# Three edits to where ScalarE's side work runs, between attention and mixing, in a fused attention, expert and mixing kernel

## The chip, the cores and the metric

The kernel runs on one core of one Trainium2 chip. The metric is the device time of one execution in microseconds (us). A core has a matrix engine (TensorE, PE in the rows), a vector engine (VectorE, DVE), a scalar engine (ScalarE, ACT), a general engine (GpSimd, POOL), and queues that issue transfers (SP's and ACT's are used here). Each engine works through its own list of instructions in the order in which they stand there; an instruction waits until what it reads is written and the buffer it writes is free, and everything behind it on its engine waits with it. TensorE writes into eight PSUM banks, which VectorE or ScalarE must read before a bank can be written again.

## The reference

Three layers follow each other: banded attention (4 batches, 8 heads, 576 positions), a mixture of 4 single-head experts over 512 channels, and a mixing layer. The change lies where the second ends and the third begins:

```
ye = a @ v @ wo[e]                       # per expert, weighted and added: x
theta = x @ w_theta
zr, zi = x * cos(theta), x * sin(theta)
y = einsum('ts,bsd->btd', w_tok_r, zr) + einsum('ts,bsd->btd', w_tok_i, zi)
u = x + y
out = u + maximum(u @ w_ch, 0)
```

The weights `w_theta`, `w_tok_*` and `w_ch` arrive as 64-bit floats and are turned into 32-bit ones on the chip.

## The kernel before

Everything is in single precision: each operand of a product is split into a high and a low part, and `mm3` (L99 to L102) issues three matmuls for one product (high by high L100, high by low L101, low by high L102). The work of a stage is written as generators that `merge` interleaves, and a scheduler then sets the final order of each engine's list from that program and its own estimate of durations; a different placement of a few instructions therefore moves many others.

The names the prediction needs, in order of time:

- `attn` (L419): expert attention of one batch and one pair of experts, in five query tiles t = 0 to 4. Scores go to bank `bs`, VectorE takes the row minimum (L452), ScalarE the exponential (L457); the scaling by the row sum and the gate (L469: `bms`, and `bpd` for the last block) is done on VectorE for one expert and on GpSimd for the other while t < 4 in the last batch. TensorE transposes the result (L480 into `bpt`, L486 into `bdt`), the copies L482 (VectorE), L484 and L490 (ScalarE) bring it back as `bpT`, and L156, L159, L498 form `o`.
- `wo` (L506): the output product of a batch into a bank `x`, eight banks per batch (two column ranges, 320 and 256 wide, by four blocks m), each copied out at L514: in batches 2 and 3 into the staging tiles `xs`, from where the SP queue writes them to DRAM. All eight copies of batch 3 are on ScalarE.
- `load64` (L107): the conversion of 64-bit weights, called with kind 0 (theta), 1 (token weights, `wtuk`, from `w64k`), 2 (channel weights, `wtuc`, from `w64c`). Its steps: first step `t` (L124 on GpSimd for kind 0, L127 on ScalarE for kinds 1 and 2), `u` (L129, ScalarE), a shift (L130) and a merge of bits (L136) on VectorE, an integer add on GpSimd (L138), the cast of the high part (L143, ScalarE) and the low part (L144: GpSimd for kind 1, VectorE for kind 2). Of nine token weights, numbers 5 to 8 are loaded late, on ScalarE's queue (L112), into two buffers in turn. `late[0]` is set in `attn(3, 1)` at t = 2 and marks the loads behind it.
- `closed[0]` is the last ScalarE cast of `attn` (L500); with kind 2 the ScalarE steps L127 and L129 are held until it has been issued.
- `theta` (L626): per batch, half and token tile i: product `th` in a `bs` bank, a transposed `x` as `xk` in a `tb` bank (L644), rounding (L648, L649, which frees `th`), sine and cosine on ScalarE (L651 to L653), the product with `xk` on VectorE (L656, which frees `xk`), and a split into `z` (high by ScalarE, low by GpSimd, L94 and L97; `cast[0]` holds the latest ScalarE half).
- `mix` (L674): `y` = `z` times token weights, four banks, nine steps c; VectorE adds each bank into `x2T` (L694). `channel` (L810) is the last product, `c`.

The stretch of the change is 276 to 345 us: `attn(3, 1)` ends, `wo(3)`, `theta(0, 0)` and then `mix(0, 0)` start. What follows until the end is the same mixing and channel work for the other halves and batches.

Of the kernel before, what the change touches and what calls it, by code (L numbers as in the profile page):

```python
# [22 lines left out]
B, H, S, D = 4, 8, 576, 64  # L23
DM = H * D
# [33 lines left out]
def kernel(ctx, tc, qT, kT, vw, consts, w_in, w_o, w_th, w_tk, w_ch, outT):  # L58
    nc = tc.nc
# [30 lines left out]
    cast = [None]  # L90
# [16 lines left out]
    def load64(kind, st, tu, dst_h, dst_l, src, scale=1.0):  # L107
# [12 lines left out]
        full = lo, hi, tu[:, 0], tu[:, 1], dst_h, dst_l  # L120
        for k in range(n):
            lo, hi, t, u, dst_h, dst_l = (x[:, step * k : step * k + step] for x in full)
            if KN["DM"][kind]:
                nc.gpsimd.tensor_scalar(out=f32(t), in0=f32(hi), scalar1=2.0**-112, scalar2=1.0, op0=ALU.mult, op1=ALU.mult)  # L124
            else:
                with tc.issue_after(closed[0].ins) if kind == 2 else nullcontext():
                    nc.scalar.mul(out=f32(t), in_=f32(hi), mul=2.0**-112)  # L127
            with tc.issue_after(closed[0].ins) if kind == 2 else nullcontext():
                nc.scalar.mul(out=u, in_=lo, mul=2.0**-29)  # L129
            shift = lambda: nc.vector.tensor_scalar(out=t, in0=t, scalar1=3, scalar2=None, op0=ALU.logical_shift_left)  # L130
            if kind == 1 and gated[0]:
                with tc.issue_after(gated[0].ins):
                    shift()
            else:
                shift()
            nc.vector.scalar_tensor_tensor(out=t, in0=hi, scalar=0x80000000, in1=t,  # L136
                                           op0=ALU.bitwise_and, op1=ALU.bitwise_or)
            nc.gpsimd.tensor_add(out=t.bitcast(I32), in0=t.bitcast(I32), in1=u.bitcast(I32))  # L138
            if scale == 1.0:
                if KN["DH"][kind]:  # L140
                    nc.vector.tensor_copy(out=dst_h, in_=f32(t))
                else:
                    nc.scalar.copy(out=dst_h, in_=f32(t))  # L143
                (nc.vector if KN["DL"][kind] else nc.gpsimd).tensor_sub(out=dst_l, in0=f32(t), in1=f32(dst_h))  # L144
            else:
                nc.scalar.activation(out=dst_h, in_=f32(t), func=AF.Copy, scale=scale)
                nc.vector.scalar_tensor_tensor(out=dst_l, in0=f32(t), scalar=scale, in1=f32(dst_h),
                                               op0=ALU.mult, op1=ALU.subtract)
# [357 lines left out]
    def wo(b):  # L506
        for n0, n1 in ((0, 320), (320, 576)):
            for m in range(NC):
                g = bank([P, n1 - n0], ("gggg", ("as", "ta", "g", "g"), ("as", "g", "ta", "g"))[KN["WB"][b]][m], f"x2{b}{m}{n0}")
                for c in range(2):  # L510
                    oh, ol = O[b, c]
                    mm3(g, woh[c][:, m * P : (m + 1) * P], wol[c][:, m * P : (m + 1) * P],
                        oh[:, n0:n1], ol[:, n0:n1], c == 0, c == 1)
                nc.scalar.copy(out=x2T[b][:, m, n0:n1] if b < 2 else xs[b][m // 2][:, m % 2, n0:n1], in_=g)  # L514
                if b > 1 and n1 == S and m % 2:
                    nc.sync.dma_start(xd[b][:, m - 1 : m + 1], xs[b][m // 2])
                yield 0.75
# [108 lines left out]
    def theta(b, dh):  # L626
        x2 = x2T[b]
        dsl = slice(dh * HW, dh * HW + HW)
        for i in range(4 if b % 2 else 5):
# [24 lines left out]
            if i < 4:  # L654
                both = ang[:, i % 2]
                d = nc.vector.tensor_mul(out=both, in0=xk.unsqueeze(1).to_broadcast([P, 2, HW]), in1=both)  # L656
                if 2 * b + dh < 3:
                    zt = slot(first[8 * b + 4 * dh + i], [P, 2, 2, HW], f"z{n}")
                    Z[b, dh, i] = zt
                    mark[b, dh, i] = d, split(zt[:, :, 0], zt[:, :, 1], both, nc.scalar, nc.gpsimd)  # L660
                elif i % 2:
                    mark[b, dh, i] = d, sums_of(b, dh, i, ang.rearrange("p j q (k n) -> p j q k n", k=2))
            else:
# [351 lines left out]
```

## Time and profile before

| what | us |
|---|---|
| runs of the kernel | 510.03, 509.95, 506.78 (median 509.95) |
| the profiled execution | 506.32 |
| its span, first to last instruction | 504.5 |
| busy in the span: TensorE | 480.7 |
| VectorE | 373.6 |
| ScalarE | 346.4 |
| GpSimd | 328.4 |

The rows further down come from the profiled execution, with times counted from the span's start. A timeline row gives start, duration, engine, line, operation and operands, and in brackets how long the engine had been idle before it and what it then waited for. A matmul's duration is its pipelined latency; successive matmuls start closer together than that. The waits view sums such idle time by pair of instructions.

### The profile page before, as it was taken

Reading aid. Unit: us, or ns where it says so; the run is one execution under the profiler, and the core shown is the slowest. Engines: PE = TensorE matmul, PEld = TensorE weight load, DVE = VectorE, ACT = ScalarE, POOL = GpSimd, SP = SyncE. Lnnn points to the kernel's source line nnn. Section 1 sums busy time; section 2 is a strip of 40 time slices with the busy share of each in tenths; the row PEclk is TensorE's granted clock in tenths of the full one; section 3 lists DMA queues with packets and bytes.
Section 4 is the critical chain, followed back from the end, with each engine's and each line's share of the span. In section 5 each row is a group of like instructions: output and inputs, shape, how many; then the busy total and the mean of one; then the engine's idle time right before and its main releaser. Section 6 shows DMA issues by size and latency. Waiting matters only on the chain.

```text
span 504.5 us, 12104 instructions
## 1 busy us (share of the span) xinstructions
PE 480.7 (95%) x4128; PEld 446.4 (88%) x4128; DVE 373.6 (74%) x1274; ACT 346.4 (69%) x1072; POOL 328.4 (65%) x455
## 2 busy tenths in 40 slices
PE   7798999999999999999999989999999999999997
PEld 5688888889998999988878778899998999999997
DVE  5766887865977868845897778987769948894942
ACT  7948787866787868858696797886177727652620
POOL 6758899764685772335784367579658926891770
PEclk9999999999999999999999999999999999999999
DMA  7564233431335342111246953231272044202002
GB/s 256 189 212 155 83 123 114 130 114 64 122 88 177 124 141 78 34 47 49 52 146 208 318 166 142 55 93 43 76 196 64 23 142 131 64 23 95 1 0 95
DMA packets 45470, 55.92 MB, mean 111 GB/s; under 512 B 6497, under 2 KB 34145, under 8 KB 45409
## 3 DMA queue, kind: packets, MB, share of 16 engines
q1 hardware_dynamic: 44544, 52.46, 33.1%
q10 hardware_dynamic: 864, 2.69, 1.5%
q8 instruction: 33, 0.54, 0.4%
q14 instruction: 29, 0.23, 0.2%
HBM read 43.34 MB, written 11.80 MB: 109 GB/s over the span
## 4 chain that ended last, share of the span: by engine, by line
PE 51%; DVE 20%; ACT 11%; POOL 9%; issue 5%; DMA 4%; SPq 0%; POOLq 0%; DVEq 0%; ACTq 0%
PE as L279 4%; PE bpt L480 3%; PE qk L100 2%; PE c L100 2%; DMA w64k<-in_dram 2%; PE qk L101 2%; PE apt L304 2%; PE c L102 2%; PE qk L102 2%; PE c L101 2%; ACT ams L292 2%; PE ao L159 2%; DMA wst<-in_dram 2%; PE bs L448 2%; DVE ang L656 2%
## 5 line engine op out<-in xcount | busy, mean ns | idle before, releaser
L292 ACT ACTIVATE ams<-ams,anm 128x128 f32<-128x128 f32 x144 | 56.6, 396 | 6.1 <-DVE anm L284 4.8
L299 POOL TENSOR_TENSOR ams<-ams,arc 128x384 f32<-128x384 f32 x48 | 40.1, 836 | 24.9 <-DVE arc L298 15.5
L87 POOL TENSOR_SCALAR QD<-qt 64x192 f32<-64x192 f32 x72 | 40.1, 557 | 19.1 <-PE as L279 11.6
L457 ACT ACTIVATE bms<-bms,bnm 64x64 f32<-64x64 f32 (+4 forms) x80 | 44.8, 562 | 9.3 <-DVE bnm L452 8.8
L279 PE MATMUL as<-kt,QD 128*128 128x128 f32 x288 | 41.9, 282 | 3.9 <-DVE anm L284 1.5
L284 DVE CUSTOM_DVE_ANT_0 ams<-as,cst 128x128 f32<-128x128 f32 x144 | 35.0, 284 | 11.5 <-PE apt L304 7.8
L279 PEld LDWEIGHTS as<-kt,QD 128*128 128x128 f32 x288 | 36.6, 193 | 7.4 <-ACT x0h L94 1.5
L452 DVE CUSTOM_DVE_ANT_0 bms<-bs,mb 64x64 f32<-64x64 f32 (+4 forms) x80 | 32.6, 424 | 7.5 <-PE bs L450 4.7
L469 POOL TENSOR_SCALAR bpd<-bms,bsm,gw 128x64 f32<-128x64 f32 (+1 forms) x47 | 21.9, 467 | 23.1 <-DVE bsm L462 10.6
L97 POOL TENSOR_TENSOR cu<-x2T,cu 128x288 fp32r<-128x288 f32 x32 | 29.1, 923 | 7.3 <-ACT cu L94 7.3
L100 PE MATMUL y<-wkh,z 128*128 128x288 f32 x108 | 32.1, 302 | 0.2 <-DVE x2T L694 0.2
L448 PE MATMUL bs<-KA,QS 128*128 128x288 f32 (+4 forms) x96 | 31.8, 340 | 0.4 <-DVE bnm L452 0.2
L101 PE MATMUL y<-wkl,z 128*128 128x288 f32 x108 | 31.9, 297 | 0.0
L102 PE MATMUL y<-wkh,z 128*128 128x288 f32 x108 | 31.3, 297 | 0.0
L768 POOL TENSOR_TENSOR x2T<-x2T,u 128x288 f32<-128x288 f32 x20 | 16.6, 839 | 21.3 <-DVE u L779 11.1
L480 PE MATMUL bpt<-cst,bms 128*128 128x128 f32 x160 | 27.6, 278 | 2.9 <-POOL bms L469 1.8
L648 ACT ACTIVATE ang<-th,magic 128x256 f32<-128x256 f32 x36 | 16.7, 466 | 17.9 <-PE th L102 17.5
L656 DVE TENSOR_TENSOR ang<-xk,ang 128x512 f32<-128x512 f32 x32 | 21.7, 684 | 8.2 <-ACT ang L653 6.2
L450 PE MATMUL bs<-KL,QS 128*128 128x288 f32 (+4 forms) x96 | 27.6, 295 | 0.1
L292 ACT ACTIVATION_READ_ACCUMULATOR ams<-ams,anm 128x1 f32 x144 | 27.5, 191 | 0.0
L820 DVE SCALAR_TENSOR_TENSOR x2T<-c,x2T 128x288 f32<-128x288 f32 x32 | 13.9, 453 | 16.5 <-PE c L102 16.3
L469 POOL TENSOR_SCALAR bms<-bms,bsm,gw 128x384 f32<-128x384 f32 (+3 forms) x40 | 25.4, 636 | 0.0
(336 smaller groups left out, 2040.5 us busy)
## 6 DMA issues: line engine op xcount, KB each, us to landing
vt<-in_dram SPq DMA_DIRECT2D x48, 192.0 KB, 3.1
or<-od SPq DMA_DIRECT2D x32, 256.0 KB, 3.3
kt<-in_dram SPq DMA_DIRECT2D x15, 320.0 KB, 3.1
qt<-in_dram SPq DMA_DIRECT2D x16, 288.0 KB, 3.4
out_dram<-x2T SPq DMA_DIRECT2D x32, 144.0 KB, 1.8
w64k<-in_dram SPq DMA_DIRECT2D x5, 576.0 KB, 3.7
od<-oh SPq DMA_DIRECT2D x8, 288.0 KB, 3.2
od<-ol SPq DMA_DIRECT2D x8, 288.0 KB, 4.1
```

What stands on the lines that cost most here:

```text
L87: nc.gpsimd.tensor_scalar(out=out, in0=in_, scalar1=by, scalar2=1.0, op0=ALU.mult, op1=ALU.mult)
L100: nc.tensor.matmul(out, wh, xh, start=first, stop=False)
L101: nc.tensor.matmul(out, wh, xl, start=False, stop=False)
L102: nc.tensor.matmul(out, wl, xh, start=False, stop=last)
L279: nc.tensor.matmul(s[:, i, :], QD[g][:, i], kt[:, 64 * blk : 64 * blk + 128], start=True, stop=True)
L284: nc.vector.tensor_tensor_reduce(out=ms[:, i, :], in0=s[:, i, :], in1=ma0 if (g == 0 and i == 0) else ma1, scale=-0.125, scalar=3.0e38, op ...
L292: nc.scalar.activation(out=ms[:, i, :], in_=ms[:, i, :], func=AF.Exp, bias=nm[:, i : i + 1], scale=-1.0, accum_out=sm[:, i, 0:1],)
L299: nc.gpsimd.tensor_mul(out=ms, in0=ms, in1=rc.unsqueeze(2).to_broadcast([P, 3, P]))
L448: nc.tensor.matmul(s[:m, : z - a], qs[:, q0 : q0 + m], ka[:, a:z], start=True, stop=False)
L457: ex = nc.scalar.activation(out=ms[:m, :w], in_=ms[:m, :w], func=AF.Exp, bias=nm[:m, ci : ci + 1], scale=-1.0, accum_out=ss[:m, i, 0:1])
L469: eng.tensor_scalar(out=dst, in0=src, scalar1=sm[:m, i : i + 1], scalar2=gw[:m, t, 2 * ep + i : 2 * ep + i + 1], op0=ALU.mult, op1=ALU.mult)
L480: nc.tensor.transpose(pt[:, jj, i, :], pn[:, i, P * j : P * j + P], ident)
```

## The change

Three edits. Of batch 3's eight output copies, the four with odd m go to VectorE. The late token weights (numbers 5 to 8) take their first step on GpSimd in place of ScalarE. And `closed[0]` is set once more at the split of the fourth tile of the first theta, so that the ScalarE steps of the channel weights' conversion are held until the cast of that `z` has been issued; before, they were held only behind the last attention cast.

```
-            if KN["DM"][kind]:
+            if KN["DM"][kind] or late[0] and kind == 1:
                 nc.gpsimd.tensor_scalar(out=f32(t), in0=f32(hi), scalar1=2.0**-112, scalar2=1.0, op0=ALU.mult, op1=ALU.mult)
             else:
                 with tc.issue_after(closed[0].ins) if kind == 2 else nullcontext():
...
-                nc.scalar.copy(out=x2T[b][:, m, n0:n1] if b < 2 else xs[b][m // 2][:, m % 2, n0:n1], in_=g)
+                dst = x2T[b][:, m, n0:n1] if b < 2 else xs[b][m // 2][:, m % 2, n0:n1]
+                if b == B - 1 and m % 2:
+                    nc.vector.tensor_copy(out=dst, in_=g)
+                else:
+                    nc.scalar.copy(out=dst, in_=g)
...
                     mark[b, dh, i] = d, split(zt[:, :, 0], zt[:, :, 1], both, nc.scalar, nc.gpsimd)
+                    if (b, dh, i) == (0, 0, 3):
+                        closed[0] = cast[0]
```

The engines' lists are alike up to the end of attention and differ from there on. Lines behind the new ones have moved: the copies of L514 are L516 (VectorE) and L518 (ScalarE) in the changed kernel, L656 is L660, L649 is L653, L644 is L648.

GpSimd while attention's last tiles run, before (`wtuk_4932` to `wtuk_4962` are the late token weights 5 to 8; `bpd_4829` and `bms_4827` are tile t = 3 of `attn(3, 1)`):

```order
L144 TENSOR_TENSOR wkl_4665<-wtuk_4932,wkh_4661 128x576
L138 TENSOR_TENSOR wtuk_4942<-wtuk_4942 128x576
L469 TENSOR_SCALAR bpd_4829<-bms_4827,bsm_4828,gw_4204 128x64
L469 TENSOR_SCALAR bms_4827<-bms_4827,bsm_4828,gw_4204 128x384
L138 TENSOR_TENSOR wtuk_4952<-wtuk_4952 128x576
```

and in the changed kernel:

```order
L144 TENSOR_TENSOR wkl_4665<-wtuk_4932,wkh_4661 128x576
L124 TENSOR_SCALAR wtuk_4952<-w64k_4951 128x576
L138 TENSOR_TENSOR wtuk_4942<-wtuk_4942 128x576
L469 TENSOR_SCALAR bpd_4829<-bms_4827,bsm_4828,gw_4204 128x64
L469 TENSOR_SCALAR bms_4827<-bms_4827,bsm_4828,gw_4204 128x384
L138 TENSOR_TENSOR wtuk_4952<-wtuk_4952 128x576
```

The first step of token weight 7 now stands ahead of the scaling of tile 3; two more such steps stand earlier, one later.

TensorE at the transposes of that same tile 3, before (`bpt_4849` and `bpt_4855` are its two banks; the first two transposes read VectorE's expert, the others GpSimd's; `x` is `wo(3)`, `th` is theta):

```order
L100 MATMUL x_4994<-oh_4265,woh_88 128x320
L101 MATMUL x_4994<-ol_4266,woh_88 128x320
L102 MATMUL x_4994<-oh_4265,wol_90 128x320
L480 MATMUL bpt_4849<-cst,bms_4827 128x128
L480 MATMUL bpt_4855<-cst,bms_4827 128x128
L480 MATMUL bpt_4849<-cst,bms_4827 128x128 x3
L480 MATMUL bpt_4855<-cst,bms_4827 128x128
```

and in the changed kernel, from the third of the twelve matmuls that now stand between the two pairs on:

```order
L100 MATMUL x_4994<-oh_4265,woh_88 128x320
L101 MATMUL x_4994<-ol_4266,woh_88 128x320
L102 MATMUL x_4994<-oh_4265,wol_90 128x320
L100 MATMUL x_4994<-oh_4671,woh_89 128x320
L100 MATMUL th_5105<-wot,or_4975 128x256
L101 MATMUL th_5105<-wot,or_4975 128x256
L102 MATMUL th_5105<-wot,or_4975 128x256
L100 MATMUL th_5105<-wot,or_4975 128x256
L101 MATMUL th_5105<-wot,or_4975 128x256
L102 MATMUL th_5105<-wot,or_4975 128x256
L480 MATMUL bpt_4849<-cst,bms_4827 128x128 x3
L480 MATMUL bpt_4855<-cst,bms_4827 128x128
```

Of the twelve, six are 320 columns wide and six 256; three of them stood ahead of the transposes before.

VectorE where the first theta's products are made, before (`ang` times `xk` is L656; `wtuc_5226` and `wtuc_5258` are the first two pieces of the channel weights):

```order
L656 TENSOR_TENSOR ang_5014<-xk_5011,ang_5014 128x512
L97 TENSOR_TENSOR ol_4672<-o_4917,oh_4671 128x128
L130 TENSOR_SCALAR wtuc_5226<-wtuc_5226 128x256
L136 SCALAR_TENSOR_TENSOR wtuc_5226<-w64ca,wtuc_5226 128x256
L656 TENSOR_TENSOR ang_5014<-xk_5091,ang_5014 128x512
L130 TENSOR_SCALAR wtuc_5258<-wtuc_5258 128x256
L136 SCALAR_TENSOR_TENSOR wtuc_5258<-w64ca,wtuc_5258 128x256
L656 TENSOR_TENSOR ang_5115<-xk_5112,ang_5115 128x512
L656 TENSOR_TENSOR ang_5115<-xk_5134,ang_5115 128x512
```

and in the changed kernel:

```order
L660 TENSOR_TENSOR ang_5014<-xk_5011,ang_5014 128x512
L97 TENSOR_TENSOR ol_4672<-o_4917,oh_4671 128x128
L660 TENSOR_TENSOR ang_5014<-xk_5091,ang_5014 128x512
L516 COPY xs3a<-x_5056 128x256
L516 COPY xs3b<-x_5073 128x256
L660 TENSOR_TENSOR ang_5115<-xk_5112,ang_5115 128x512
L660 TENSOR_TENSOR ang_5115<-xk_5134,ang_5115 128x512
L130 TENSOR_SCALAR wtuc_5226<-wtuc_5226 128x256
L136 SCALAR_TENSOR_TENSOR wtuc_5226<-w64ca,wtuc_5226 128x256
L130 TENSOR_SCALAR wtuc_5258<-wtuc_5258 128x256
L136 SCALAR_TENSOR_TENSOR wtuc_5258<-w64ca,wtuc_5258 128x256
```

Four instructions of the conversion left the row of products, two output copies came in.

## Rows read from the trace of the kernel before

**Rows 1.** Waits of TensorE, 276 to 345 us: total, times, longest
```profile
PE bpt L480 <- POOL bms L469: 1.3, 1, 1.3
PE xk L644 <- DVE ang L656: 1.1, 1, 1.1
PE th L100 <- DVE ang L649: 0.7, 1, 0.7
...
PE y L100 <- DVE x2T L694: 0.2, 1, 0.2
```

**Rows 2.** Waits of TensorE, 345 us to the end: first and last of six
```profile
PE c L100 <- DVE zf L670: 1.3, 1, 1.3
...
PE ya L100 <- DVE x2T L694: 0.3, 1, 0.3
```

**Rows 3.** Windows: us, busy time of PE, PEld, DVE, ACT, POOL, clock, DMA
```profile
276.00:310.00 34.00, 31.02 (x225) 26.16 (x222) 26.36 (x64) 28.93 (x74) 18.35 (x18) 1.00 0.65 227
310.00:328.00 18.00, 17.13 (x132) 16.71 (x131) 17.33 (x30) 13.90 (x39) 11.26 (x12) 1.00 0.19 57
```

**Rows 4.** Prices: one line's instructions, min/median/max ns, first and last start
```profile
L514 ACT COPY xs3a<-x x4: 425/433/467, 300.1 to 306.6; 128x320 f32<-128x320 f32 x2, 128x256 f32<-128x256 f32 x2
L127 ACT ACTIVATE wtuk<-w64k x4: 719/731/755, 281.6 to 297.7; 128x576 f32<-128x576 f32 x4
L124 POOL TENSOR_SCALAR wtut<-w64t x4: 656/665/681, 72.9 to 177.6; 128x512 f32<-128x512 f32 x4
```

**Rows 5.** Timeline, 290.7 to 293.2 us: the transposes of tile 3
```profile
289.37 1.43 POOL L138 TENSOR_TENSOR wtuk<-wtuk 128x576 int32<-128x576 int32 x1
289.43 1.58 DVE L469 TENSOR_SCALAR bms<-bms,bsm,gw 128x384 f32<-128x384 f32 x1
...
290.78 0.78 POOL L469 TENSOR_SCALAR bpd<-bms,bsm,gw 128x64 f32<-128x64 f32 x1
...
291.55 1.16 POOL L469 TENSOR_SCALAR bms<-bms,bsm,gw 128x384 f32<-128x384 f32 x1
...
292.76 0.66 PE L480 MATMUL bpt<-cst,bms 128*128 128x128 f32 x4 [1.26 <-POOL bms L469]
```

**Rows 6.** Chain that ended last, 276 to 300 us: token weight 7's transfer
```profile
283.94 5.77 DMA w64k<-in_dram
```

**Rows 7.** Timeline of TensorE, two theta matmuls behind each other
```profile
294.07 0.28 PE L101 MATMUL th<-wot,or 128*128 128x256 f32 x1
294.18 0.28 PE L102 MATMUL th<-wot,or 128*128 128x256 f32 x1
```

**Rows 8.** Timeline of VectorE, 293 to 297 us
```profile
293.01 1.15 DVE L469 TENSOR_SCALAR bpd<-bms,bsm,gw 128x64 f32<-128x64 f32 x1
294.07 0.41 DVE L482 COPY bpT<-bpt 128x256 f32<-128x256 f32 x1
294.40 1.37 DVE L469 TENSOR_SCALAR bms<-bms,bsm,gw 128x512 f32<-128x512 f32 x1
295.70 0.30 DVE L469 TENSOR_SCALAR bpd<-bms,bsm,gw 128x64 f32<-128x64 f32 x1
295.92 0.54 DVE L469 TENSOR_SCALAR bms<-bms,bsm,gw 128x512 f32<-128x512 f32 x1
```

**Rows 9.** Timeline, 307.2 to 309.4 us: the stop early in the first mix
```profile
306.92 1.41 DVE L136 SCALAR_TENSOR_TENSOR wtuc<-w64ca,wtuc 128x256 uint32<-128x256 uint32 x1
...
308.98 0.44 PE L644 MATMUL xk<-cst,xt 128*128 128x128 f32 x2 [1.05 <-DVE ang L656]
```

**Rows 10.** Timeline, 323.5 to 327.7 us: the stop late in the first mix
```profile
323.59 1.20 DVE L130 TENSOR_SCALAR wtuc<-wtuc 128x256 uint32<-128x256 uint32 x1
324.83 1.39 DVE L136 SCALAR_TENSOR_TENSOR wtuc<-w64c,wtuc 128x256 uint32<-128x256 uint32 x1
326.14 0.41 DVE L649 SCALAR_TENSOR_TENSOR ang<-ang,th 128x256 f32<-128x256 f32 x1
...
326.61 0.39 PE L100 MATMUL th<-wot,xo 128*128 128x256 f32 x1 [0.70 <-DVE ang L649]
```

## What I expect of the change

> **What bounds the kernel now.** I first looked at the windows of the stretch that the change touches. From 276 to 310 us TensorE is busy 31.0 of 34 us and ScalarE 28.9; from 310 to 328 us TensorE is busy 17.1 of 18 us and VectorE 17.3 [rows 3]. So TensorE's stream of matmuls sets the time, and an edit to other engines is worth only what TensorE waits for them. The waits view gives that directly: up to 345 us the waits to look at are 1.3 us for GpSimd's scaling of attention tile 3, 1.1 us for a theta product on VectorE, 0.7 us for a rounding on VectorE and 0.2 us for an added bank [rows 1]. Behind 345 us there are six kinds of wait, the longest 1.3 us and the shortest 0.3 us [rows 2]; the edits touch none of that work, only its order. What can be won is a few us of 506, what can be lost likewise.
>
> Then I read each of the three large waits in the timeline. At 291.2 us TensorE has done two of six transposes of tile 3 and stops 1.26 us until GpSimd has scaled the other expert [rows 5]. At 307.8 us it stops 1.05 us, since VectorE ran a piece of the channel weights (L136, 1.41 us) ahead of the theta product that would free the bank [rows 9]. At 325.9 us it stops 0.70 us, since VectorE ran L130 and L136 of a later piece (1.20 and 1.39 us) ahead of the rounding that frees the theta bank [rows 10].
>
> **The output copies.** Four of eight leave ScalarE, 4 x 0.43 = 1.7 us [rows 4]. On VectorE the trace shows no copy of an output bank; the nearest is the copy of a 256-column PSUM bank, 0.41 us [rows 8], and in proportion 0.51 us for 320 columns, so 2 x 0.41 + 2 x 0.51 = 1.8 us. I cost them at nothing: between 276 and 310 us VectorE is idle 34 - 26.4 = 7.6 us [rows 3]. Without that cover the two that stand between the theta products would add 0.8 us to the theta products behind them, whose first reader on TensorE comes some 27 matmuls into the mix.
>
> **The first step of the token weights.** ScalarE loses 4 x 0.73 = 2.9 us [rows 4]. GpSimd gains four instructions. The nearest row is the same line at 512 columns, 0.665 us [rows 4]; at 576 columns that is 0.75 us each, 3.0 us in all. Total load is no matter, GpSimd has 34 - 18.4 = 15.6 us free [rows 3]; the place is. The step of weight 7 now stands ahead of the integer add of weight 6 and of tile 3's scaling. Its transfer lands at 283.94 + 5.77 = 289.7 us [rows 6], so it ends at 290.5; the add (1.43) ends at 291.9; the two L469 take 0.78 + 1.16 = 1.9 us as before, or about 1.1 us if VectorE does not hold them up (VectorE's own pair at these sizes takes 0.30 and 0.54, and I allow GpSimd a third more). The tile is ready at 293.0 to 293.8 us, in place of 292.7.
>
> Against that, TensorE now has twelve matmuls between the two pairs of transposes. A 256-column one takes 294.18 - 294.07 = 0.11 us of stream [rows 7], a 320-column one 0.14 in proportion; six of each are 1.5 us, of which three wide ones (0.4 us) stood ahead of the pair before. TensorE thus comes to the GpSimd half 1.1 us later than at 291.4, at 292.5, and waits 0.5 to 1.3 us there in place of 1.26. **Term: -0.3 us** (bounds -0.8 and 0).
>
> VectorE pays next. Its shift of weight 7 waits for GpSimd's step (290.5), and the score minimum of tile 4, the two roundings and the merge stand behind it, some 3 us, so the four scalings of tile 4 begin at about 293.6. The copy of tile 3's second bank, which stood among them at 294.07 [rows 8], now stands behind all four. Alone these take 2 x (0.30 + 0.54) = 1.7 us; as in rows 8, with two of four held up, 1.15 + 1.37 + 0.30 + 0.54 = 3.4 us. The copy ends at 295.7 to 297.4. TensorE wants it at 293.4 + transposes, one theta tile and seven matmuls (2.2 us) = 295.6. **Term: +0.8 us** (bounds 0 and +1.8).
>
> Weight 8's transfer is now issued on ScalarE's queue behind weight 7's L129 and the first rounding of theta, about 290.9 in place of 287.9. By weight 7's 5.77 us [rows 6] it lands at 296.7; GpSimd, busy till then with tile 3 and weights 6 and 7, wants it at about that time, and its user in the mix is the last of nine steps, some 20 us on. Cost nothing.
>
> **The hold on the channel weights.** No instruction is added. ScalarE's L127 and L129 of the first pieces, and with them VectorE's L130 and L136, come behind all four theta products. At 307.8 us the product no longer stands behind a 1.41 us L136, and the reader of its bank stands later in TensorE's list. **Term: -1.05 us** (bounds -1.05 and 0). The same shift carries pieces 6 and 7 behind the first mix's end: L130 and L136 of piece 6 (1.20 + 1.39 us) no longer stand ahead of the rounding at 326.14 [rows 10], and the adding of the banks finds VectorE free. **Terms: -0.70 and -0.2 us** (bounds 0 each). The pieces must be made all the same; they move to 328 us and on, and their first reader is the channel product after 345 us.
>
> One rule weighs against this. By the trace, VectorE and GpSimd hold each other up: L469 of 384 columns took 1.58 us beside GpSimd's L138 [rows 5], one of 512 columns 0.54 us elsewhere [rows 8]. The Trainium skill (SBUF — State Buffer, Who interferes with whom) says that the two share a pair of ports, which the one that issues first keeps for its whole instruction while the other fully blocks; the two rows agree with that. By that rule alone each of the four new GpSimd steps could block a VectorE instruction, a loss of up to four times 0.75 us, an estimate, where my sum puts only the +0.8.
>
> **Sum.** -0.3 + 0.8 - 1.05 - 0.70 - 0.2 = -1.45 us. The profiled execution took 506.32 us, 1.8 more than its span; 506.32 - 1.45 = 504.9 us. The median of the three runs, 509.95, lies 3.6 us above the profiled execution and the lowest run, 506.78, beside it; I see nothing that says on which of the two levels a new median falls, so the upper one gives 508.5 and I put the number midway, at 506.7 us.
>
> **The rivals.** *Given back.* The stops before 328 us go, but the order behind 345 us, which differs everywhere, makes as many new ones: one more stop of the size of the longest there, 1.3 us [rows 2], takes the gain, 506.3 us (midway 508.1). For: VectorE must still make the moved pieces between 328 and 345 us. Against: those windows have room there that 310 to 328 us lacks.
>
> *More than the sum.* The waits for GpSimd and for the copy are both hidden (-0.8 and 0), the three VectorE stops go (-1.95), and the longest stop behind 345 us, 1.3 us, goes with the new order: -4.0 us, 502.3 (midway 504.1). For: each is a wait for one instruction that a few matmuls cover. Against: it needs the early place to come out at its best bound.
>
> *Slower: GpSimd in VectorE's way.* While VectorE scales tile 4, GpSimd has five instructions in a row (adds, low parts, the step of weight 8). If all four scalings are held up, as two were [rows 8], they take 2 x (1.15 + 1.37) = 5.0 us, the copy ends at 299.0, and TensorE waits 3.4 us for it. With -0.3 and -1.95 that is +1.2: 507.5 us (midway 509.3). It decides from the point where the copy ends later than 295.6 + 2.25 = 297.9. For: the row of 1.58 us. Against: before, with GpSimd as busy, two of four were held up. By the skill's rule this is what a lock held for whole instructions would do; no other number hangs on that sentence.
>
> **How the numbers follow.** The forecast gets 0.55, given back 0.18, more 0.13, slower 0.14. The range: at best -4.0 on the lower level, 502.3; at worst +1.2 on the upper level, 511.2. Cutting about a tenth at either end, where a rival and one of the two levels have to meet, leaves 502.8 to 510.0. About 1% (5 us) is what a measurement of this kernel can tell from no change. Faster by that means under 504.85 against the shown median: half of the forecast's lower-level half (0.14), most of the lower-level half of more (0.07) and a little of given back, 0.23. Slower means over 515, which no case reaches; 0.05 for what I do not see. The same: 0.72.
>
> **What would show it.** Right: no wait of TensorE for L660 in the first 10 us of mix, none for L653 at its end, GpSimd's L469 of tile 3 ending at 293 to 294 us, and VectorE less than 17 us busy in the 18 us before the first mix ends. Wrong in a step: a TensorE stop over 2 us at `o` of tile 3 (the copy term), a stop at `z` of the first mix (the output copies were not free), a stop in the channel product (the pieces came too late), or stops behind 345 us that differ by over 1.5 us in sum from before.

## The result, and the profile after

The changed kernel took 513.04 us (median of 9 runs, 510.18 to 515.28), the kernel before 507.14 us beside it (median of 9, 506.72 to 510.03): the ratio of the means is 1.0101, 95% interval 1.007 to 1.0132. It is slower by 1%; I had forecast 506.7 us and no change, with a chance of 0.05 for this side.

The profiled execution took 514.29 us, its span 512.4 us, against 506.32 and 504.5 before. To see where the time went I read in both timelines where a tile's first matmul starts (`woT` holds the transposed output weights, the first of the work that leads to theta):

| first (and last) matmul of | before | after | late by |
|---|---|---|---|
| `woT` | 274.1 | 276.4 | 2.3 |
| `th` | 285.8 | 289.1 | 3.3 |
| `xk` | 303.8 | 311.0 | 7.2 |
| `y` | 306.9 | 313.6 | 6.7 |
| `c` | 346.0 | 351.4 | 5.4 |
| last `c` | 500.9 | 508.8 | 7.9 |

The first 2.3 us arise before `woT`, where both programs are the same, so they belong to these two executions and not to the change. Of the other 5.6 us, 1.0 + 3.9 are lost between `woT` and `xk`, 0.5 + 1.3 = 1.8 are won from `xk` to the channel product `c`, and 2.5 are lost behind it. TensorE's waits in the changed kernel, 278 to 351 us (engine, tile and line that waited, what it waited for: us in total, times, longest), answer to [rows 1]:

```profile
PE o L156 <- DVE bpT L482: 2.0, 1, 2.0
PE th L100 <- DVE bnm L452: 1.2, 1, 1.2
PE th L100 <- ACT wot L94: 0.7, 1, 0.7
PE bs L448 <- DVE bnm L452: 0.6, 1, 0.6
PE y L100 <- DVE x2T L700: 0.3, 1, 0.3
PE th L100 <- DVE ang L653: 0.3, 1, 0.3
```

The stops of 1.3 us for GpSimd's scaling, 1.1 for the theta product and 0.7 for the rounding at the mix's end are gone, as forecast (the 0.3 us for a rounding, L653, lie later, at 344.8 us). The one for the added bank stayed, 0.3 us in place of 0.2. In their place stand a stop of 2.0 us at `o` and 1.2 + 0.6 us for score minima (L452). Behind 351 us, the same view answers to [rows 2], six kinds and 3.3 us in sum before, eight kinds and 5.0 us now:

```profile
PE yb L100 <- ACT W L612: 1.3, 2, 0.9
PE c L100 <- DVE ang L660: 0.9, 1, 0.9
PE ya L100 <- DVE x2T L700: 0.8, 1, 0.8
...
PE xk L648 <- DVE ang L660: 0.2, 1, 0.2
```

The windows of the stretch [rows 3] (start:end, length, busy time of TensorE, its weight loads, VectorE, ScalarE and GpSimd, granted clock, DMA share, GB/s):

```profile
278.00:289.90 11.90, 10.20 (x63) 8.09 (x59) 7.35 (x21) 6.00 (x17) 4.62 (x7) 1.00 0.85 292
289.90:296.70 6.80, 6.02 (x28) 5.74 (x30) 5.32 (x15) 4.11 (x11) 3.08 (x4) 0.50 0.52 175
...
315.00:333.00 18.00, 17.66 (x138) 17.48 (x138) 14.70 (x30) 14.70 (x40) 12.26 (x13) 1.00 0.26 88
```

From 289.9 us TensorE runs for 6.8 us at clock 0.50, that is 1.2 in place of 2.4 GHz; in the profile before there is no such stretch while TensorE works. It was busy 6.02 us of it; at twice the clock that is about 3.0 us of work, so by this estimate the slow stretch cost up to 3.0 us, more than any one stop. The last row, the end of the first mix, has VectorE busy 14.70 of 18 us, where it was 17.33.

Two timelines show the stops (start, duration, engine, line, operation, operands; in brackets the idle time ahead and what was waited for). The first is the score minimum:

```profile
287.86 0.71 POOL L124 TENSOR_SCALAR wtuk<-w64k 128x576 f32<-128x576 f32 x1 [1.87 <-DVE bnm L452]
...
288.54 1.40 POOL L138 TENSOR_TENSOR wtuk<-wtuk 128x576 int32<-128x576 int32 x1
288.60 1.65 DVE L130 TENSOR_SCALAR wtuk<-wtuk 128x576 uint32<-128x576 uint32 x1 [0.41 <-POOL wtuk L124]
...
290.18 0.45 DVE L452 CUSTOM_DVE_ANT_0 bms<-bs,mb 128x288 f32<-128x288 f32 x1
...
290.68 0.58 PE L100 MATMUL th<-wot,or 128*128 128x256 f32 x1 [1.25 <-DVE bnm L452]
```

GpSimd ends the moved step of weight 6 and goes straight on to the integer add of weight 5 (L138). VectorE's shift (L130) waits for the step, so it can begin only when the add has just begun, 0.06 us behind it, and takes 1.65 us, in place of 0.45 in a run below, where no add stands beside it ([rows 5] shows the like on L469). The score minimum behind the shift is late, and TensorE stops 1.25 us. The clock falls in the middle of that stop. The second is tile 4, on VectorE:

```profile
299.84 0.79 DVE L469 TENSOR_SCALAR bpd<-bms,bsm,gw 128x64 f32<-128x64 f32 x1
300.55 1.71 DVE L469 TENSOR_SCALAR bms<-bms,bsm,gw 128x512 f32<-128x512 f32 x1
302.18 0.69 DVE L469 TENSOR_SCALAR bpd<-bms,bsm,gw 128x64 f32<-128x64 f32 x1
302.79 0.53 DVE L469 TENSOR_SCALAR bms<-bms,bsm,gw 128x512 f32<-128x512 f32 x1
303.24 0.41 DVE L482 COPY bpT<-bpt 128x256 f32<-128x256 f32 x1
```

and on GpSimd and TensorE:

```profile
299.16 1.42 POOL L138 TENSOR_TENSOR wtuk<-wtuk 128x576 int32<-128x576 int32 x1 [0.75 <-DVE wtuk L136]
300.54 1.44 POOL L144 TENSOR_TENSOR wkl<-wtuk,wkh 128x576 fp32r<-128x576 f32 x1
302.07 0.76 POOL L124 TENSOR_SCALAR wtuk<-w64k 128x576 f32<-128x576 f32 x1
...
303.80 0.29 PE L156 MATMUL o<-bpT,vg 128*64 128x128 f32 x1 [2.04 <-DVE bpT L482]
```

The scalings take 0.79 + 1.71 + 0.69 + 0.53 us; the first three begin beside a GpSimd instruction (L138, L144, L124). The copy comes behind them and TensorE waits for it 2.04 us.

### The profile page after: what moved, and what is told of

It reads as the page before. It is cut to its first block, busy times and chain, and to the rows that moved or that the text cites. A ratio compares the mean times of both kernels' runs of the same rounds, so it can differ in the third digit from the quotient of the medians.

```text
span 512.4 us, 12104 instructions
## 1 busy us (share of the span) xinstructions
PE 483.6 (94%) x4128; PEld 449.5 (88%) x4128; DVE 375.5 (73%) x1278; ACT 342.3 (67%) x1064; POOL 329.5 (64%) x459
## 5 line engine op out<-in xcount | busy, mean ns | idle before, releaser
L452 DVE CUSTOM_DVE_ANT_0 bms<-bs,mb 64x64 f32<-64x64 f32 (+4 forms) x80 | 32.5, 422 | 7.1 <-PE bs L450 4.5
L469 POOL TENSOR_SCALAR bpd<-bms,bsm,gw 128x64 f32<-128x64 f32 (+1 forms) x47 | 21.8, 465 | 23.0 <-DVE bsm L462 10.6
L102 PE MATMUL y<-wkh,z 128*128 128x288 f32 x108 | 31.4, 299 | 0.0
L94 ACT CAST cu<-x2T 128x288 fp32r<-128x288 f32 x32 | 13.2, 428 | 22.4 <-PE c L102 10.4
L660 DVE TENSOR_TENSOR ang<-xk,ang 128x512 f32<-128x512 f32 x32 | 21.7, 682 | 5.8 <-ACT ang L657 3.6
L304 PE MATMUL apt<-cst,ams 128*128 128x128 f32 x144 | 24.3, 278 | 1.6 <-POOL ams L299 1.4
L469 POOL TENSOR_SCALAR bms<-bms,bsm,gw 128x384 f32<-128x384 f32 (+3 forms) x40 | 25.1, 627 | 0.0
```

The source lines that it names most:

```text
L102: nc.tensor.matmul(out, wl, xh, start=False, stop=last)
L452: nc.vector.tensor_tensor_reduce(out=ms[:m, a:z], in0=s[:m, : z - a], in1=mb[:m, mo + a : mo + z], scale=-0.125, scalar=nm[:m, 0:1] if ci ...
L469: eng.tensor_scalar(out=dst, in0=src, scalar1=sm[:m, i : i + 1], scalar2=gw[:m, t, 2 * ep + i : 2 * ep + i + 1], op0=ALU.mult, op1=ALU.mult)
```

## The experiments

All ratios are of means, against the kernel before run on the same chip, with a 95% interval; most kernels had 10 to 12 runs. The table has all of them. The middle columns come from one profiled execution of each, so that transfers and a clock that fell in that one count in them too: from the first `woT` to the first `xk` (end of attention and theta), from there to the first `c`, and from the first to the last `c`. The last column counts the runs in which the mean granted clock was 0.999 or more.

| run | ratio | `woT`-`xk` | `xk`-`c` | `c`-`c` | full clock |
|---|---|---|---|---|---|
| kernel before | 1 | 29.7 | 42.2 | 154.9 | 86 of 146 |
| the change | 1.0101 [1.0070, 1.0132] | 34.6 | 40.4 | 157.4 | 0 of 9 |
| x_hold_alone | 0.9988 [0.9966, 1.0010] | 30.1 | 41.7 | 155.1 | 8 of 12 |
| x_copies_alone | 1.0009 [0.9983, 1.0035] | 29.4 | 41.9 | 155.9 | 10 of 12 |
| x_step_alone | 1.0062 [1.0028, 1.0096] | 31.9 | 42.0 | 155.6 | 1 of 10 |
| x_without_copies | 1.0047 [1.0012, 1.0082] | 31.4 | 41.7 | 155.0 | 5 of 10 |
| x_without_step | 1.0015 [0.9994, 1.0037] | 33.2 | 40.4 | 158.5 | 5 of 10 |
| x_without_hold | 1.0100 [1.0073, 1.0127] | 31.4 | 41.8 | 156.7 | 1 of 4 |
| x_copy_first | 1.0025 [1.0002, 1.0048] | 31.6 | 40.4 | 157.4 | 4 of 12 |
| x_shift_late | 1.0114 [1.0084, 1.0145] | 33.8 | 42.0 | 157.5 | 0 of 6 |
| x_copy_and_shift | 1.0109 [1.0079, 1.0139] | 33.7 | 42.8 | 157.5 | 0 of 5 |
| x_adds_first | 1.0049 [1.0022, 1.0077] | 30.5 | 40.4 | 157.4 | 3 of 12 |
| x_wide_copies | 1.0016 [0.9992, 1.0039] | 32.7 | 41.7 | 155.1 | 6 of 12 |
| x_hold_wide_copies | 1.0006 [0.9987, 1.0026] | 29.3 | 41.7 | 155.1 | 5 of 12 |
| x_adds_first_wide | 1.0014 [0.9986, 1.0042] | 35.6 | 41.7 | 155.0 | 4 of 12 |
| x_adds_first_no_copies | 1.0041 [1.0011, 1.0071] | 36.6 | 41.7 | 155.0 | 3 of 12 |
| x_adds_first_one_table | 0.9972 [0.9949, 0.9994] | 32.1 | 41.7 | 155.0 | 10 of 12 |
| x_one_table_no_copies | 0.9961 [0.9940, 0.9981] | 30.0 | 41.7 | 155.0 | 11 of 12 |
| x_all_in_order | 1.0005 [0.9986, 1.0024] | 29.0 | 40.4 | 157.5 | 10 of 12 |

**One edit, and two.** The first six runs below have one or two of the change's three edits, with the lines of its diff as they stand. The step alone:

```
-            if KN["DM"][kind]:
+            if KN["DM"][kind] or late[0] and kind == 1:
```

> Before with the third edit alone (first step of token weights 5 to 8 on GpSimd). Theory A (this step is what costs: GpSimd's next integer add takes hold ahead of VectorE's shift, the score minimum behind the shift comes late, TensorE stops at about 287 to 291 us and then runs at a granted clock of 0.5 for some us): slower than before by 2.5 to 6 us, mean clock 0.997 or less, the shifts of weights 6 to 8 at 1.1 to 1.7 us each instead of 0.45 to 0.75. Theory B (the output copies on VectorE cost) and theory C (the hold on the channel weights costs, by the new order of everything behind it): within 1.5 us of before, clock 0.999.

> The changed kernel without its third edit: copies on VectorE and the hold, the first step of weights 5 to 8 back on ScalarE. Theory A: 0 to 2 us faster than before, clock 0.999, no stop of TensorE over 1 us between 285 and 292 us (before's own times). Theory B or C: as slow as the changed kernel, 3 to 6 us over before.

> The changed kernel without the hold on the channel weights: copies on VectorE, first step on GpSimd. Theory A: 3 to 7 us slower than before (the cost stays, the gain of the hold, some 2 us, is missing). Theory B: 3 to 6 us slower too, but with VectorE's copies in TensorE's waits. Theory C: within 1.5 us of before.

> The changed kernel with all eight output copies on ScalarE again: first step on GpSimd and the hold. Theory A: as slow as the changed kernel, 3 to 6 us over before, clock 0.997 or less. Theory B: within 1.5 us of before, clock 0.999. Theory C: as slow as the changed kernel.

The hold alone:

```
+                    if (b, dh, i) == (0, 0, 3):
+                        closed[0] = cast[0]
```

> The kernel before with the second edit alone: ScalarE's first two steps of the channel weights stand behind the last rounding copy of the first theta, not behind the attention's. By the terms of my sum the stops for the theta product (1.05 us), for the rounding at the mix's end (0.70) and for the added bank (0.2) go, and nothing else moves: ratio 1 - 1.95 / 507 = 0.996, faster. Rival (given back): the stops go, but as many new ones come behind 345 us, ratio 0.999 to 1.002.

The copies alone:

```
...
+                if b == B - 1 and m % 2:
+                    nc.vector.tensor_copy(out=dst, in_=g)
...
```

> The kernel before with the first edit alone: four of batch 3's eight output copies on VectorE. My sum costed them at nothing: ratio 1.000. Theory D (the copies cost nothing where they stand, but the instruction order behind 345 us that comes with them loses, since all four kernels with these copies took 156.7 to 158.5 us from the first to the last channel product and all without them 154.9 to 155.6): the stretch from the first to the last channel product takes 156.5 to 158 us and the ratio is 1.002 to 1.005, with no loss ahead of the first channel product.

Every kernel with the step on GpSimd is slower, from 1.0047 to 1.0101, and stops at `o` for 1.7 to 2.0 us; the three without it lie at 0.9988, 1.0009 and 1.0015, and none of them stops there for the copy. So the step carries most of the loss, as theory A has it, with misses. x_without_step was not faster than before, and its profile has a stop of 1.6 us for a cast of `wot` at 287 us, where I expected none over 1 us. x_without_copies lost 2.4 us, not 3 to 6, and its profiled execution kept the full clock. In x_step_alone the shifts of weights 6 to 8 took 1.62, 0.45 and 1.65 us, not all of them over 1.1.

The hold alone wins nothing that can be told from no change, against 0.996 expected. Its profile still has the stop for the rounding at the end of the first mix:

```profile
326.94 0.39 PE L100 MATMUL th<-wot,xo 128*128 128x256 f32 x1 [0.92 <-DVE ang L649]
```

VectorE now runs another piece of the conversion ahead of that rounding, the low part L144 (1.30 us from 325.25). The copies alone cost 1.0 us behind the first `c` in the profile and nothing that the times show, which misses the 1.6 to 3.1 us that I expected there. The middle column gives what the sum had promised, 40.4 in place of 42.2 us, in the kernels with the hold and all four copies together, unless the shifts are moved too; either edit alone gives only 0.3 to 0.5.

**The copy of tile 3 back among the scalings.** In the changed kernel, tile 4's scalings are held behind that copy:

```
+                        mid[0] = nc.vector.tensor_copy(out=pT[:, j0 : j0 + jn], in_=pt[:, :jn])
...
+                    tail = (b, ep, t) == (3, 1, 4) and eng is nc.vector
+                    with tc.issue_after(mid[0].ins) if tail else nullcontext():
```

> The changed kernel with one order more: VectorE's copy of tile 3's second bank (L482 there) stands ahead of tile 4's four scalings (L469), as it did before the change among them. Nothing else moves on VectorE, ScalarE and GpSimd; on TensorE one output product of 256 columns moves up by two rows. Theory A (the copy behind four scalings is the mis-sized term of my sum): the stop of TensorE at o for the copy, 2.0 us in the changed kernel, falls under 0.5 us, and the ratio to the kernel before falls from 1.010 by about 2.0 / 508 = 0.004, to 1.006. Rival B (the copy only receives a delay that GpSimd made earlier, so that TensorE stops at another place): another stop of 1 to 2 us comes up within the next 5 us, and the ratio stays at 1.009 to 1.010.

One row moves on VectorE and one group of three matmuls on TensorE. Its waits of TensorE, 275 to 346 us:

```profile
PE x L100 <- ACT oh L94: 1.1, 1, 1.1
PE th L100 <- DVE bnm L453: 0.8, 1, 0.8
PE x L100 <- DVE bnm L453: 0.7, 1, 0.7
```

The stop at `o` is gone and the ratio falls from 1.0101 to 1.0025, by 3.9 us, more than the 2.0 us of the stop. The rival, the same stop elsewhere, falls in the main, though 1.1 + 0.7 us at `x` are new. So the place of that copy alone carries 3.9 us of the loss. How much of it is the stop and how much the clock (full in four of twelve runs, in place of none of nine) this run does not tell.

**The shifts behind the score minima,** alone and with the copy's order:

```
-                with tc.issue_after(gated[0].ins):
+                with tc.issue_after(smin[0].ins if late[0] else gated[0].ins):
...
+                    smin[0] = nc.vector.tensor_tensor_reduce(
```

> The changed kernel, with VectorE's shifts of the late token weights (L130) put behind the last score minimum (L452) of attention tile 4, so that no score minimum stands behind a shift that waits for GpSimd. Theory A (the shift, held 1.65 us beside GpSimd's integer add, keeps the score minimum back, TensorE stops 1.2 us for the bank and its granted clock falls behind that stop): no stop of TensorE at th for L452, the shifts beside an add still take over 1 us, the granted clock stays 1.0 from 285 to 300 us, and the ratio falls from 1.010 to 1.003 to 1.007 (1.2 us of stop, and some 2 us if the clock stays up). Rival B (the loss is the copy behind tile 4's scalings alone, and the clock only noise): the ratio stays at 1.009 to 1.010. Rival C (the later shifts collide with tile 4's scalings and cost as much there): the stop at o grows over 3 us.

> Both orders together: shifts behind the score minima, and the copy of tile 3's second bank ahead of tile 4's scalings. Theory A: with both stops gone and the clock kept, what is left is the predicted gain of the hold, so the ratio is 0.997 to 1.002. Rival B (GpSimd's step costs what it costs through the total of VectorE and GpSimd in this stretch, wherever the instructions stand): the ratio stays at 1.006 to 1.010, with other stops.

The waits of the first, 278 to 352 us:

```profile
PE th L100 <- DVE ang L654: 2.5, 2, 1.7
PE bpt L481 <- DVE bms L470: 2.1, 2, 1.4
PE o L156 <- ACT wtuk L129: 1.1, 1, 1.1
```

No score minimum is waited for now, but 5.7 us of other stops stand there, and the ratios stay at 1.0114 and 1.0109. Theory A's forecast for both fails. But these runs do not show what the shift costs, for the new order brought something else. ScalarE loads three function tables, where the changed kernel loads one, since theta's first sine has slipped ahead of tile 4's exponential (L458). ScalarE and VectorE in x_shift_late:

```profile
291.41 1.28 ACT L656 ACT_TABLE_LOAD   x1
...
293.29 1.28 ACT L458 ACT_TABLE_LOAD   x1
...
296.25 1.28 ACT L656 ACT_TABLE_LOAD   x1
...
298.36 0.42 DVE L654 SCALAR_TENSOR_TENSOR ang<-ang,th 128x256 f32<-128x256 f32 x1 [1.90 <-ACT ang L653]
```

The longest stop, 1.7 us at `th`, is for that rounding (L654), whose ScalarE half stands behind the third load. x_copy_and_shift has the same three loads and the same stop. TensorE's list moved in many other places as well, so the price of the score minimum's stop by itself stays open.

**The add ahead of the next step.** GpSimd's step of a weight is put behind the integer add of the weight before:

```
+                with tc.issue_after(added[0].ins) if late[0] and added[0] else nullcontext():
                     nc.gpsimd.tensor_scalar(out=f32(t), in0=f32(hi), scalar1=2.0**-112, ...)
...
+            if kind == 1 and late[0]:
+                added[0] = add
```

> The changed kernel with one order more on GpSimd: the first step of a late token weight (L124) stands behind the integer add (L138) of the weight before it, so that the add no longer follows the step at once, beside VectorE's shift (L130) of the same weight. Theory P (VectorE's shift is held for the whole of a GpSimd add that was issued just ahead of it): the shifts of weights 6 and 7, 1.65 us each in the changed kernel, take 0.45 to 0.75 us. The score minimum behind the shift of weight 6 then ends at about the same place, since the step itself comes 0.7 to 1.4 us later, so the ratio moves by less than 0.003 from 1.010. Rival (the shift is long for a reason of its own, its operands or the transfers landing): it still takes over 1 us with no add beside it.

VectorE and GpSimd in that run:

```profile
285.10 0.71 POOL L125 TENSOR_SCALAR wtuk<-w64k 128x576 f32<-128x576 f32 x1
...
287.07 0.45 DVE L131 TENSOR_SCALAR wtuk<-wtuk 128x576 uint32<-128x576 uint32 x1
...
292.18 0.71 POOL L125 TENSOR_SCALAR wtuk<-w64k 128x576 f32<-128x576 f32 x1
...
292.92 0.46 DVE L131 TENSOR_SCALAR wtuk<-wtuk 128x576 uint32<-128x576 uint32 x1 [0.82 <-POOL wtuk L125]
...
296.06 0.54 DVE L473 TENSOR_SCALAR bms<-bms,bsm,gw 128x512 f32<-128x512 f32 x1
296.52 0.31 DVE L473 TENSOR_SCALAR bpd<-bms,bsm,gw 128x64 f32<-128x64 f32 x1
```

With no add beside it the same shift takes 0.45 us, not 1.65, and tile 4's scalings 0.31 and 0.54 us each. That a shift is held up by a GpSimd add issued just ahead of it is thus shown: the same instruction on the same operands, with no GpSimd instruction running beside it. The Trainium skill (SBUF — State Buffer, Who interferes with whom) says this of the one that comes second, where both engines need the ports that they share. The hold-up did not vanish but moved: the merge of bits behind the first of these shifts then took 1.67 us, beside GpSimd's low part (L147). The ratio fell by 0.0052, more than I expected. The copy of tile 3 also came ahead of the scalings with the new order, and ScalarE has three table loads here too; this run does not part these.

**The order behind the channel product.** The two copies of 256 columns go back to ScalarE, first in the kernel with the copy's order, then in the one without the step:

```
-                if b == B - 1 and m % 2:
+                if b == B - 1 and m % 2 and n0 == 0:
```

> The changed kernel with VectorE's copy of tile 3's second bank ahead of tile 4's scalings, as in the run named x_copy_first, and of the four output copies only the two of 320 columns on VectorE; the two of 256 columns go back to ScalarE. Behind the first mix the order of every engine is then that of the kernel without the copies. Theory D: the stretch from the first to the last channel product falls from 157.4 us to 155.0, and the ratio from 1.0025 to 0.998. Rival (the copies cost through VectorE's time where they stand): half of the copies gives back half of their cost, about 0.8 us, and the later stretch keeps over 156.5 us: ratio 1.001.

> The hold and the two copies of 320 columns on VectorE, with the first step of the token weights left on ScalarE: the second and half of the first edit. Theory D and theory A together (the step on GpSimd costs about 1.7 us through the copy behind tile 4's scalings, the later order 2.4 us): compared with the run without the step, 1.0015, the later order's 2.4 us come back, so 0.997, at best a little faster than the kernel before. Rival (nothing but the hold counts): 0.999, as with the hold alone.

Without these two copies the engines' order behind the first mix is that of x_without_copies, and `c`-`c` falls from 157.4 to 155.1 us, as forecast; their work lies some 40 us earlier, so it is the order that loses. `W` is an operand of a later mix product, `yb`. VectorE in a later batch, in the changed kernel:

```profile
438.66 0.69 DVE L660 TENSOR_TENSOR ang<-xk,ang 128x512 f32<-128x512 f32 x1
439.27 0.41 DVE L653 SCALAR_TENSOR_TENSOR ang<-ang,th 128x256 f32<-128x256 f32 x1
439.60 0.70 DVE L609 TENSOR_TENSOR s<-ang 128x256 f32<-128x256 f32 x1
440.33 1.41 DVE L610 TENSOR_TENSOR s<-s,ang 128x256 f32<-128x256 f32 x1
```

and in x_without_copies:

```profile
431.29 0.86 DVE L605 TENSOR_TENSOR s<-ang 128x256 f32<-128x256 f32 x1
432.18 0.91 DVE L606 TENSOR_TENSOR s<-s,ang 128x256 f32<-128x256 f32 x1
```

In the first a rounding (L653) stands ahead of the sums that make `W`, and TensorE waits for `W` at `yb`, 1.3 us in all; in the second no rounding stands there and that wait is missing. In time this pair left the cost open: 1.0025 and 1.0016, with overlapping intervals. So did x_hold_wide_copies, 1.0006 in place of 0.997.

**Both causes away.** What was still open then, and its two runs:

> The changed kernel with GpSimd's first step of a late token weight behind the integer add of the weight before, as in the run x_adds_first, and of the output copies only the two of 320 columns on VectorE. If the two causes make up the whole loss, no stop of TensorE between 284 and 305 us is over 1 us, the first channel product comes about 1 us earlier after woT than before (70.9 us in place of 71.9), the stretch from the first to the last channel product takes 155.1 us, and the ratio is 0.997 to 0.999, which is what my sum said without its copy term (1 - 1.45 / 507 = 0.997). If a third cause is missing, the ratio stays at 1.001 to 1.005.

> The kernel before with the hold and the first step on GpSimd, that step behind the integer add of the weight before, and all output copies left on ScalarE. If the two causes make up the whole loss: ratio 0.997 to 0.999, as in the run beside it, since the wide copies cost nothing where they stand. If the wide copies help ScalarE by their 2 x 0.43 us and more where it is waited for, this run is 1 to 2 us slower than the one beside it. If a third cause is missing: 1.001 to 1.005.

`c`-`c` is 155.0 us in both, but the ratios are 1.0014 and 1.0041: a third cause was missing. ScalarE in the first, with VectorE and TensorE behind it:

```profile
292.18 0.75 ACT L130 ACTIVATE wtuk<-w64k 128x576 uint32<-128x576 uint32 x1 [1.94 <-DMA w64k<-in_dram]
...
293.46 1.28 ACT L659 ACT_TABLE_LOAD   x1
...
295.67 1.28 ACT L461 ACT_TABLE_LOAD   x1
296.96 0.77 ACT L461 ACTIVATE bms<-bms,bnm 128x576 f32<-128x576 f32 x1
...
297.86 0.16 DVE L465 TENSOR_REDUCE bsm<-BS 128x2 f32<-128x4 f32 x1 [3.22 <-ACT bms L461]
298.15 1.28 ACT L659 ACT_TABLE_LOAD   x1
...
299.02 0.49 PE L502 MATMUL o<-bpT,VD 128*128 128x128 f32 x2 [1.87 <-DVE bpT L492]
```

Here too theta's first sine has slipped ahead of tile 4's exponential, so ScalarE loads a table for the sine, one for the exponential, and a third for the sines after it. The changed kernel and the kernel before load one in this stretch, so this cause is no part of the change's own loss: it came in with the new order on GpSimd. With a transfer that came late on top, VectorE waits 3.22 us for the exponential and TensorE 1.87 us at `o`. In their runs at full clock these two kernels took 507.96 and 508.26 us (medians of 4 and 3) and the kernel before 508.19 (of 12): what they lose, they lose in the runs below it.

**One table load.** Theta's sine is put behind the last exponential, in both of these kernels; then with all three edits:

```
+                final[0] = ex
...
+            with tc.issue_after(final[0].ins):
                 nc.scalar.activation(out=sn, in_=rn, func=AF.Sin, scale=-TWO_PI)
```

> The kernel of the run x_adds_first_wide with one order more: theta's first sine stands behind the last exponential of the attention, so that ScalarE loads activation tables once in this stretch and not three times. If the two loads (2 x 1.28 us, on a ScalarE that is busy 18.7 of 19 us there) are the missing third cause: tile 4's exponential is not 3 us behind, no stop of TensorE at o over 1 us, and the ratio falls from 1.0014 to 0.996 to 0.998. Rival (they are hidden, and the rest is the granted clock and transfers that land late in some executions): 1.000 to 1.002.

> The same with all output copies on ScalarE, as in the run x_adds_first_no_copies (1.0041). If the table loads are the third cause: 0.996 to 0.999. If ScalarE's load is, which the two wide copies lighten by 0.87 us: 0.002 above the run beside it. Rival: 1.002 to 1.004, as without the order.

> The changed kernel, all three edits, with the two orders (GpSimd's first step behind the add of the weight before; theta's first sine behind the last exponential). It differs from x_adds_first_one_table (0.9972) in the two copies of 256 columns on VectorE. Theory D (they bring the later order that loses 2.3 us between the first and the last channel product): 0.9972 + 2.3 / 508 = 1.0017 (0.9995 to 1.0035), with 157.4 us between these products. Rival (that order costs nothing in time): 0.995 to 0.999.

0.9972 and 0.9961, both wholly below 1: the order with three loads was the third cause, and the forecasts of 0.996 to 0.998 and to 0.999 hold. In each pair ScalarE's order, three of TensorE's matmuls and at most one VectorE instruction differ. The third pair, x_adds_first and x_all_in_order, goes the same way (1.0049 to 1.0005); only in the pair without copies do the intervals not overlap. x_one_table_no_copies, with the hold, the step on GpSimd and the two orders, is the fastest kernel here, 506.35 us median (504.70 to 508.04) against 508.74. The one table load left in it, and TensorE's longest waits from 275 to 347 us:

```profile
294.07 1.28 ACT L658 ACT_TABLE_LOAD   x1
```

```profile
PE th L100 <- DVE ang L655: 1.2, 2, 0.9
PE x L100 <- ACT xs3a L520: 0.8, 1, 0.8
```

No single stop there reaches 1 us. Nor do the wide copies, which lighten ScalarE, make the run beside it faster. x_all_in_order has the narrow copies in addition: 157.5 us of `c`-`c` again and 1.0005 in place of 0.9972, as expected of the later order. The difference is 0.0033 or 1.7 us; the profiles give 1.2 (1.3 us won at `xk`-`c`, 2.5 lost behind it). The two intervals overlap a little, so a cost of that order in time is likely, its size not settled.

## Why the prediction was wrong, step by step

The sum said -1.45 us; in the profile 5.6 us were lost behind the first `woT`.

**The copy of tile 3: the mis-sized term.** I named the row, its place and its waiter, and gave +0.8 us between 0 and 1.8. It measured 2.04 us in the profile and 3.9 us in time when taken away. The range rested on two of four scalings held up, 3.4 us in sum [rows 8]; three were held up, and they took 3.72. I took a value in the middle, although the row of 1.58 us [rows 5] showed what a GpSimd add does to a scaling and I had counted five GpSimd instructions there.

**GpSimd in VectorE's way, beyond that place: left out.** I costed the new steps by GpSimd's free time and their own 0.71 to 0.76 us, close to the 0.75 that I had worked out. What I did not ask is what GpSimd does next. A step that releases VectorE and is followed at once by an add makes VectorE come second. In the changed kernel that happened twice, to the shifts of weights 6 and 7, 1.65 us each in place of 0.45; behind the first stood the score minimum, for which TensorE stopped 1.25 us. My slower rival had this mechanism, but at tile 4's scalings alone, with +1.2 us and a chance of 0.14; the estimate of up to four times 0.75 us, which I set beside the sum, was nearer than the sum. The add cost more than the step: the shifts lost 1.2 us each.

**The transfer of weight 7.** I had it land at 289.7 us. In the changed kernel ScalarE issued it at 287.94, in place of 283.94 us before [rows 6], and used it at 295.02 with 1.66 us of waiting; tile 3's scaling on GpSimd, which I put at 293 to 294 us, ended at 298.4. The stop for that scaling went all the same, 1.26 us where the sum had 0.3, since TensorE was later than GpSimd. (Before, it began at 291.5 us, not at 291.2 as I read it; nothing hangs on that.)

**The three stops of the first mix: right in size, not in cause.** Two of the three went, that for the added bank did not (0.3 us), and `xk` to `c` is 1.8 us shorter, where the sum had 1.95. But not by the hold: with it alone the rounding was waited for 0.92 us, and the stretch became only 0.5 us shorter. Hold and copies are needed together, and with the narrow copies comes the loss behind `c`.

**Given back: right in kind, too small.** One stop of 1.3 us was the rival (its sum gives 506.2 us, not the 506.3 that I wrote); the change lost 2.5 us there, and its stops grew by 1.7 us in sum, past the 1.5 that I had named as a sign.

**The clock: not in any case of mine.** In runs of one kernel the time often goes with the granted clock: x_adds_first_wide took 507.24 to 508.27 us in its four runs at 1.0, and 512.48 to 513.07 in three at 0.992 or 0.993. It does not always: x_hold_alone's longest run, 511.42 us, was at 1.0. The change had none of nine runs at full clock, the kernel before 86 of 146. In its profile the clock fell while TensorE stood still for the score minimum; where the stops of over 1 us in that stretch went (x_one_table_no_copies), eleven of twelve runs stayed at full clock. Every fall of the clock that the profiles show while TensorE worked came in a stop of over 1 us or a few us behind one. Yet the stops of 2.0 us at `o` in x_without_copies and x_without_hold had none behind them, and in four profiles the clock fell at 64 us, far ahead of the edits. That the stops bring the clock down is how it looks; no run held TensorE busy through a stop, so it is not shown. Nor is the step's loss all clock: in runs at full clock x_without_copies took 508.81 us (median of 5), the kernel before beside it 507.50 (of 15).

**The level.** I put the number midway between two levels. The 146 runs of the kernel before go from 506.14 to 511.86 us without two levels that stand apart. On the lower level alone, 504.9, I would have missed by more.

## What to carry to other kernels

When work moves to GpSimd, look at what GpSimd does right behind the moved instruction: if that instruction releases VectorE, the next GpSimd instruction can start first and hold VectorE up, here by 1.2 us. Then read who is queued behind the held instruction, not how busy the two engines are. And where a scheduler orders the program, compare its order far behind the edit and the table loads on ScalarE too: here two order constraints took the kernel with the hold and the step from a ratio of 1.0047 to 0.9961, and two copies brought another order, 2.3 us longer, some 40 us behind them.

## What the runs showed of the hardware that I had not expected

The same shift of 128x576 took 0.45 us alone and 1.65 us when it began 0.06 us behind a GpSimd add of 1.40. The first transfer of the late token weights, issued where the two programs are still alike, took 5.2 us from issue to use in the changed kernel's profile (280.03 to 285.20) and 3.9 in that of the kernel before (277.72 to 281.62), and ScalarE, which issues and waits for them in order, passed that on. One table load of ScalarE took 1.28 us in every profile.
